# Gated linear attention, mixture of experts and a second layer on one core: k's decay and the weights' splitting on VectorE, the state's decay on ScalarE, and a fifth late unit of layer 2

## The chip, the core and the metric

The kernel runs on one core of a Trainium2 chip. TensorE (PE) multiplies matrices and loads its weights over a side path (PEld). VectorE (DVE), ScalarE (ACT) and GpSimd (POOL) work on tiles in SBUF or on PE's results in PSUM, and SyncE (SP) issues transfers. Each engine takes its instructions in the order of the program and waits on semaphores for the others. The metric is the device time of one execution in microseconds (us).

## The reference, cut to what matters

```python
# q, k, v, alpha: (4, 8, 768, 48)
for t in range(S):
    state = alpha[:, :, t, :, None] * state + einsum('bhd,bhe->bhde', k[:, :, t], v[:, :, t])
    y[:, :, t] = einsum('bhd,bhde->bhe', q[:, :, t], state)
x = y as (3072, 384)
# experts: only rows with x @ w_skip > 0
logits = x @ w_gate                   # 8 experts, the best one is taken
x = x + gate * (relu(x @ w1[e]) @ w2[e])      # 384 -> 1024 -> 384
# second layer, all rows
h = x @ w_in                          # 384 -> 2048
out = (h - tanh(h)) @ w_out           # 2048 -> 384
```

All of it is wanted to fp32 accuracy.

## The kernel before

**Attention.** The sequence is cut into 6 chunks of 128 steps, and with 4 batches that makes 24 units, one for each call of `astep(s)`. For unit s + 2 DVE scans the decay forward (`F`, L196) and backward (`G`, L203). POOL multiplies q by F (`qh`, L209), k by G (`kh`, L214) and makes `pf` (L218), the decay over the whole chunk. For unit s PE makes the scores `pa` (`mmA`, L226), which DVE masks (`am`, L231); it transposes `kh` (`trk`, L255), which ACT copies to `kt` (L261); it sums y in `py` from the old state (`mmYs`, L240) and from `am` (`mmYa`, L247); and it sums the new state in `pd` (`mmS`, L271 and L274). DVE multiplies `pd` by `pf` and so writes the state `st` (`evst`, L282), two instructions of 64 partitions for each unit. ACT copies y (`xT`, L288), PE transposes it back beside the routing scores (`mmX`, L295), and ACT copies both out (L303, L304). Routing sorts the rows of 12, 8 and 4 units by expert, and POOL's indirect transfers scatter them to `xb` in memory (L414).

**Weights.** PE multiplies rounded fp32 numbers, so every weight is split into a rounded high part (`wh`, by ACT) and the rest (`wl`), and each product is made of three. A unit is a 128x1536 block: 64 units are the experts', 16 are layer 2's. An expert's unit takes two operations: `wh` on ACT (L141), and `wl` (L144) on DVE, or on POOL for every fourth unit. A unit of layer 2 comes in 64 bits and takes seven: `cs` and `ca` on DVE (L155, L156), `cl` on ACT (L159), `cs` on DVE (L160), `wh` on ACT (L162), two multiplications and subtractions on POOL (L166, L167) and `wl` on DVE (L170). These four groups are called s0 to s3 in `wsplit`. Five units of layer 2 are split beside the attention, seven beside the experts, and the last four ("late") in the first steps of layer 2.

**Tail of attention, experts and layer 2.** Between attention and experts the first five units of layer 2 are already used for block 0. The experts' loop takes one unit in each step: `mm1` (L559, into `hp`), `hh` on ACT, `hl` on DVE (L564), and `mm2` two steps later (L577 to L579). Layer 2 goes over 6 blocks of 512 rows by 16 units less the five done: `mm1b` (L463, into `h`), then `g` by ACT and DVE (L469, L471), `gh` on ACT (L473), `gl` on DVE (L475), and two steps later `mm2b` (L497). Results leave by indirect transfers (L511).

The order is written by hand: lists `at` and `aft` hold what is to be issued ahead of a step and behind it, and every engine keeps that order.

Of the kernel before, what the change touches and what calls it, by code (L numbers as in the profile page):

```python
# [19 lines left out]
C = 128  # L20
# [22 lines left out]
NE0 = 5  # L43
NLATE = 4

# [15 lines left out]
@with_exitstack  # L61
def tile_kernel(ctx: ExitStack, tc: tile.TileContext, att0, att, vz, wsg, wmoe, wff, out):
    nc = tc.nc
# [62 lines left out]

    def wsplit(i, eng=None):
# [313 lines left out]
    def split2(nb, a, pt=None):  # L441
        d = X2[nb]
        if a == 0:
# [242 lines left out]
    def astep(s):  # L686
# [22 lines left out]
        if ok(s + 2):  # L709
            scanF(s + 2)  # L710
            mkqh(s + 2)
        trk(s)
        evk(s)
        if ok(s - 2):
            mmX(s - 2)
            evxa(s - 2)
        if ok(s - 1):
            mmYs(s - 1)
        mask(s)
        if ok(s - 1):  # L720
            evst(s - 1)
            mmYa(s - 1)
# [71 lines left out]
    for f in range(NE0):  # L794
# [7 lines left out]
        if f == NE0 - 1:  # L802
# [152 lines left out]
def layout(inputs):  # L955
# [24 lines left out]
    def units(w_in, w_out):  # L980
# [34 lines left out]
```

## Time and profile before

| | us |
|---|---|
| runs | 768.1, 770.59, 770.76 (median 770.59) |
| profiled execution | 771.64 |
| its span in the trace | 769.9 |
| PE busy | 696.4 (90%) |
| DVE busy | 473.5 (62%) |
| ACT busy | 280.8 (36%) |
| POOL busy | 257.2 (33%) |

The shares are averages over stages that look nothing alike. The span is best read in these stretches: the start up to 35.3 us, attention in its steady loop up to 163.5, its end with the routing and block 0's first part up to 212.85, the experts up to 365.86, layer 2 while its late units are split up to about 408, and layer 2 to the end. The rows below name each stage's engines with their busy time.

### The profile page before, as it was taken

To read this page: it belongs to the slowest core of one execution; us is meant where nothing else is said; L and a number is where in the kernel's file an instruction comes from. 1 tells how busy PE (TensorE), PEld (TensorE's weight loads), DVE (VectorE), ACT (ScalarE), POOL (GpSimd) and SP (SyncE) were. 2 spreads that over 40 slices of the span, in tenths; PEclk is the share of its full clock that TensorE was granted. 3 is DMA by queue.
4 is the path that set the end of the run, shared out by engine and by line. 5 is a ranking of instruction groups with operands and counts; after the bars stand their busy time and mean duration, and the time that the engine had idled before them with its cause. 6 is when DMAs were issued, how large, how long until landed. Compare 5 with 4: busy or idle time off the path is not lost.

```text
span 769.9 us, 11892 instructions
## 1 busy us (share of the span) xinstructions
PE 696.4 (90%) x4707; PEld 635.0 (82%) x4707; DVE 473.5 (62%) x698; ACT 280.8 (36%) x508; POOL 257.2 (33%) x196
## 2 busy tenths in 40 slices
PE   4788878857899998999999999999999999999993
PEld 3677767746798888989888989999989899989993
DVE  7999999883779988983775333433333343434331
ACT  2323313212475655663343333333333332333221
POOL 6687657954536754551430100200020020002002
PEclk9999989989999999999999999999999999999997
DMA  9899746524477876861311101100110020001001
GB/s 270 220 278 277 185 93 184 148 82 145 136 279 244 271 252 215 268 206 71 98 42 42 42 0 42 42 1 0 42 42 1 10 74 1 1 0 42 1 1 44
DMA packets 31598, 84.55 MB, mean 110 GB/s; under 512 B 4437, under 2 KB 12661, under 8 KB 31536
## 3 DMA queue, kind: packets, MB, share of 16 engines
q1 hardware_dynamic: 27440, 71.80, 31.5%
q0 software_dynamic: 4096, 11.92, 4.3%
q8 instruction: 39, 0.64, 0.4%
q14 instruction: 23, 0.19, 0.1%
HBM read 67.02 MB, written 17.43 MB: 110 GB/s over the span
## 4 chain that ended last, share of the span: by engine, by line
issue 47%; DVE 29%; PE 14%; POOL 4%; ACT 2%; DMA 2%; another core or an unknown queue 1%; POOLq 0%; DVEq 0%; ACTq 0%
DVE wl L144 5%; DVE F L196 4%; DVE G L203 4%; PE hp L559 4%; DVE am L231 2%; POOL out_dram L511 2%; DVE wl L170 2%; DVE st L282 1%; DVE hl L564 1%; DVE cs L155 1%; PE y L497 1%; PE pa L226 1%; PE yp L577 1%; DVE ca L156 1%; PE yp L579 1%
## 5 line engine op out<-in xcount | busy, mean ns | idle before, releaser
L471 DVE TENSOR_TENSOR g<-h,g 128x512 f32<-128x512 f32 x96 | 66.3, 691 | 161.4 <-ACT g L469 152.2
L511 POOL DMA_INDIRECT out_dram<-ob,id x24 | 23.4, 977 | 335.4 <-DVE ob L510 308.7
L497 PE MATMUL y<-wh,gl 128*128 128x384 f32 x384 | 131.0, 341 | 3.3 <-DVE gl L475 2.8
L497 PE MATMUL y<-wh,gh 128*128 128x384 f32 x384 | 130.2, 339 | 0.0
L497 PE MATMUL y<-wl,gh 128*128 128x384 f32 x384 | 130.1, 339 | 0.0
L475 DVE TENSOR_TENSOR gl<-g,gh 128x512 fp32r<-128x512 f32 x96 | 78.2, 814 | 65.9 <-ACT gh L473 44.0
L469 ACT ACTIVATE g<-h 128x512 f32<-128x512 f32 x96 | 57.3, 598 | 168.2 <-PE h L463 166.0
L463 PE MATMUL h<-xh,wh 128*128 128x512 f32 x288 | 115.5, 401 | 1.0 <-DVE g L471 1.0
L463 PE MATMUL h<-xl,wh 128*128 128x512 f32 x288 | 113.9, 395 | 0.0
L463 PE MATMUL h<-xh,wl 128*128 128x512 f32 x288 | 113.8, 395 | 0.0
L473 ACT CAST gh<-g 128x512 fp32r<-128x512 f32 x96 | 59.6, 620 | 83.4 <-DVE g L471 83.1
L497 PEld LDWEIGHTS y<-wh,gl 128*128 128x128 f32 x384 | 72.6, 189 | 5.2 <-DVE gl L475 5.1
L497 PEld LDWEIGHTS y<-wl,gh 128*128 128x128 f32 x384 | 72.6, 189 | 4.2
L497 PEld LDWEIGHTS y<-wh,gh 128*128 128x128 f32 x384 | 72.6, 189 | 3.9
L463 PEld LDWEIGHTS h<-xl,wh 128*128 128x128 f32 x288 | 54.3, 189 | 12.5
L559 PE MATMUL hp<-eh,wh 128*128 128x256 f32 x192 | 56.8, 296 | 8.4 <-DVE hl L564 8.0
L141 ACT CAST wh<-raw 128x768 fp32r<-128x768 f32 x64 | 53.4, 835 | 26.6 <-PE yp L579 18.5
L463 PEld LDWEIGHTS h<-xh,wh 128*128 128x128 f32 x288 | 54.3, 188 | 10.6 <-DVE g L471 1.9
L463 PEld LDWEIGHTS h<-xh,wl 128*128 128x128 f32 x288 | 54.5, 189 | 8.6
L144 DVE TENSOR_TENSOR wl<-raw,wh 128x768 fp32r<-128x768 f32 x45 | 61.2, 1360 | 0.0
L559 PE MATMUL hp<-eh,wl 128*128 128x256 f32 x192 | 53.8, 280 | 0.0
L559 PE MATMUL hp<-el,wh 128*128 128x256 f32 x192 | 53.7, 280 | 0.0
(139 smaller groups left out, 1273.3 us busy)
## 6 DMA issues: line engine op xcount, KB each, us to landing
raw<-in_wmoe_dram SPq DMA_DIRECT2D x64, 384.0 KB, 3.6
raw<-in_wff_dram SPq DMA_DIRECT2D x16, 768.0 KB, 4.9
it<-in_att_dram SPq DMA_DIRECT2D x40, 289.5 KB, 7.0
vt<-in_vz_dram SPq DMA_DIRECT2D x24, 256.0 KB, 3.0
xb<-zero SPq DMA_DIRECT2D x6, 776.0 KB, 10.7
rows<-xb SPq DMA_DIRECT2D x6, 776.0 KB, 4.4
xe<-xb SPq DMA_DIRECT2D x8, 388.0 KB, 4.7
it<-in_att_dram SPq DMA_DIRECT2D x2, 772.0 KB, 9.5
```

What stands on the lines that cost most here:

```text
L141: A.copy(t_["h"], raw_t[i])
L144: (eng or V).tensor_tensor(t_["l"], raw_t[i], t_["h"].bitcast(F32), ALU.subtract)
L196: V.tensor_tensor_scan(flat(d["F"]), d["it"][:, :NP * C], flat(ind), 0.0, ALU.mult, ALU.add)
L203: V.tensor_tensor_scan(flat(d["G"])[:, ::-1], d["it"][:, 1:NP * C + 1][:, ::-1], flat(d1s[u % 2])[:, ::-1], 0.0, ALU.mult, ALU.add)
L463: T.matmul(hp, *todo.pop(0), start=len(todo) == last, stop=not todo)
L469: A.activation(g, hp, AF.Tanh)
L471: V.tensor_tensor(g, hp, g, ALU.subtract)
L473: A.copy(gh, g)
L475: V.tensor_tensor(gl, g, gh.bitcast(F32), ALU.subtract)
L497: T.matmul(o, g_[:, sl_], w_[:, DM:], start=first and n == 0, stop=last and n == len(todo) - 1)
L511: s_ = nc.gpsimd.indirect_dma_start(out[:, :], bass.IndirectOffsetOnAxis(d["id"][:, a:a + 1], 0), ob, None, bounds_check=N - 1, oob_is_err ...
L559: T.matmul(hp, w_[:, ks], x_[:, k], start=n == 0, stop=n == 3 * KT - 1)
```

## The change

`kh` is made by DVE instead of POOL. `pf` stays on POOL, now directly behind `qh` (`mkpf`). All `wl` of the experts and both operations of s2 are on DVE, so that POOL keeps `qh`, `pf` and the indirect transfers. `evst` leaves DVE: ACT multiplies `pd` by the column of `pf`, four activations of 128x112 for each unit. For that `pd` and the two `py` become PSUM tiles that are zeroed once and stay, and v is no longer padded from 48 to 64 columns. In a step `mmYs(s - 1)` comes ahead of `trk(s)`, and `evst(s - 1)` ahead of `evk(s)`. The zeros of `xb` are written by four transfers at steps 6 to 9 instead of six at steps 2 to 7. Beside the experts six units of layer 2 are split, one for every nine steps, instead of seven, one for every seven; five are late, with s2 and s3 in the same step.

```diff
-NLATE = 4
+NLATE = 5
@@ wsplit
         def n1():
-            (eng or V).tensor_tensor(t_["l"], raw_t[i], t_["h"].bitcast(F32), ALU.subtract)
+            V.tensor_tensor(t_["l"], raw_t[i], t_["h"].bitcast(F32), ALU.subtract)
...
         def s2():
             a_ = t_["a"].bitcast(F32)
-            G.tensor_tensor(t_["f"], t_["f"], t_["s"].bitcast(F32), ALU.mult)
-            G.tensor_tensor(a_, a_, t_["h"].bitcast(F32), ALU.subtract)
+            V.tensor_tensor(t_["f"], t_["f"], t_["s"].bitcast(F32), ALU.mult)
+            V.tensor_tensor(a_, a_, t_["h"].bitcast(F32), ALU.subtract)
@@ mkkh
-        G.tensor_tensor(d["kh"], d["kk"], d["G"], ALU.mult)
+        V.tensor_tensor(d["kh"], d["kk"], d["G"], ALU.mult)
+
+    def mkpf(u):
+        d = U[u]
@@ evst
-            for j in range(2):
-                r = slice(HP * j, HP * j + HP)
-                V.tensor_tensor(st[u % B][r, :, HP * j:HP * j + D], d["pd"][r],
-                                d["pf"][r].unsqueeze(2).to_broadcast([HP, NP, D]), ALU.mult)
+            for p in range(NP):
+                A.activation(st[u % B][:, p, :HP + D], pd[:, p, :HP + D], AF.Copy, scale=d["pf"][:, p:p + 1])
@@ astep
         if ok(s + 2):
             scanF(s + 2)
             mkqh(s + 2)
+            mkpf(s + 2)
+        if ok(s - 1):
+            mmYs(s - 1)
         trk(s)
+        if ok(s - 1):
+            evst(s - 1)
         evk(s)
...
-        if ok(s - 1):
-            mmYs(s - 1)
         mask(s)
         if ok(s - 1):
-            evst(s - 1)
             mmYa(s - 1)
@@ stages beside the experts
-        stage(NMU + r, 7 * (r - NE0) + 5, None, max(0, 7 * (r - NE0) + -1))
+        stage(NMU + r, 9 * (r - NE0) + 5, max(0, 9 * (r - NE0) - 1))
@@ late units
-        for n, f_ in zip((0, 0, 1, 2), wsplit(r)):
+        for n, f_ in zip((0, 0, 1, 1), wsplit(r)):
```

Three places show how it moves instructions. First DVE in an attention step that carries a part of a layer-2 unit. Before:

```order
L196 SCALAR_TENSOR_TENSOR F_1007<-it_97,ind 128x512
L197 RECIPROCAL d_1_105<-F_1007 128x4
L231 TENSOR_TENSOR am_1031<-pa_996,maskT 128x1024
L282 TENSOR_TENSOR st_124<-pd_979,pf_835 64x4x48 x2
L203 SCALAR_TENSOR_TENSOR G_1043<-it_97,d_0_104 128x512
L160 TENSOR_SCALAR cs_974<-ca_975 128x768
L196 SCALAR_TENSOR_TENSOR F_1082<-it_98,ind 128x512
```

DVE after, in a step of the same kind:

```order
L196 SCALAR_TENSOR_TENSOR F_722<-it_97,ind 128x512
L197 RECIPROCAL d_0_104<-F_722 128x4
L234 TENSOR_TENSOR am_751<-pa_711,maskT 128x1024
L203 SCALAR_TENSOR_TENSOR G_761<-it_97,d_0_104 128x512
L214 TENSOR_TENSOR kh_763<-it_97,G_761 128x512
L160 TENSOR_SCALAR cs_689<-ca_690 128x768
L166 TENSOR_TENSOR cl_691<-cl_691,cs_689 128x768
L167 TENSOR_TENSOR ca_690<-ca_690,wh_767 128x768
L196 SCALAR_TENSOR_TENSOR F_798<-it_98,ind 128x512
```

The two `st` are gone from DVE; `kh` stands directly behind G, and L166 and L167 between L160 and the next F.

Second, ACT in an attention step. Before:

```order
L288 COPY xT_861<-py_814 128x512
L261 COPY kt_873<-pk_868 128x512
L303 COPY xr_316<-px_875 128x384
L304 COPY l_317<-px_875 128x36
L288 COPY xT_930<-py_882 128x512
```

ACT after:

```order
L289 COPY xT_796<-py_128 128x512
L284 ACTIVATE st_121<-pd,pf_581 128x112 x4
L264 COPY kt_818<-pk_809 128x512
L304 COPY xr_326<-px_820 128x384
```

Four activations that write the state now stand between `xT` and `kt`.

Third, DVE in two steps of layer 2 with a late unit (`g_8`, `g_9` are the units' numbers). Before:

```order
L471 TENSOR_TENSOR g_8_4335<-h_0_8_4325,g_8_4335 128x512
L475 TENSOR_TENSOR gl_8_4337<-g_8_4335,gh_8_4336 128x512
L448 COPY id_4356<-rows_2903 128x4
L439 TENSOR_TENSOR xl_1_4355<-px_0_4358,xh_1_4354 128x3x128
L170 TENSOR_TENSOR wl_4288<-ca_4281,cl_4282 128x768
L155 TENSOR_SCALAR cs_4367<-raw_4365 128x768
L156 SCALAR_TENSOR_TENSOR ca_4368<-raw_4365,cs_4367 128x768
L160 TENSOR_SCALAR cs_4367<-ca_4368 128x768
L471 TENSOR_TENSOR g_9_4387<-h_0_9_4377,g_9_4387 128x512
L475 TENSOR_TENSOR gl_9_4389<-g_9_4387,gh_9_4388 128x512
```

DVE after:

```order
L155 TENSOR_SCALAR cs_4352<-raw_4350 128x768
L156 SCALAR_TENSOR_TENSOR ca_4353<-raw_4350,cs_4352 128x768
L160 TENSOR_SCALAR cs_4352<-ca_4353 128x768
L472 TENSOR_TENSOR g_9_4372<-h_0_9_4362,g_9_4372 128x512
L476 TENSOR_TENSOR gl_9_4374<-g_9_4372,gh_9_4373 128x512
L166 TENSOR_TENSOR cl_4354<-cl_4354,cs_4352 128x768
L167 TENSOR_TENSOR ca_4353<-ca_4353,wh_4359 128x768
L170 TENSOR_TENSOR wl_4360<-ca_4353,cl_4354 128x768
L472 TENSOR_TENSOR g_10_4404<-h_0_10_4394,g_10_4404 128x512
```

L166 and L167 now stand on DVE ahead of L170, and all three ahead of the second step's `g`, not behind its `gl`.

## Rows read from the trace of the kernel before

**Rows 1.** Windows: length, busy (instructions) of PE, PEld, DVE, ACT, POOL, clock, DMA, GB/s.

```profile
35.30:163.50 128.20, 99.07 (x1234) 89.88 (x1235) 123.24 (x157) 37.09 (x81) 96.22 (x72) 0.93 0.70 185
...
212.85:365.86 153.01, 144.63 (x1004) 138.88 (x1004) 128.03 (x167) 88.51 (x155) 76.77 (x43) 1.00 0.68 225
365.86:408.30 42.44, 40.90 (x199) 34.69 (x199) 32.14 (x41) 18.28 (x30) 16.80 (x10) 1.00 0.20 63
```

**Rows 2.** Timeline of an attention step: start, duration, engine, line, operation, idle before.

```profile
65.98 1.16 PE L226 MATMUL pa<-qh,kh 64*128 64x128 f32 x16
...
66.31 1.43 POOL L214 TENSOR_TENSOR kh<-it,G 128x512 f32<-128x512 f32 x1 [2.09 <-DVE G L203]
66.53 2.30 DVE L196 TENSOR_TENSOR_SCAN F<-it,ind 128x512 f32<-128x512 f32 x1
...
69.08 1.23 DVE L231 TENSOR_TENSOR am<-pa,maskT 128x1024 f32<-128x1024 f32 x1
...
72.00 1.16 PE L226 MATMUL pa<-qh,kh 64*128 64x128 f32 x16
```

**Rows 3.** DVE's groups in 35.3:163.5: count, busy us, mean ns, idle before.

```profile
L196 DVE TENSOR_TENSOR_SCAN F<-it,ind 128x512 f32<-128x512 f32 x18 | 37.7, 2094 | 0.0
L203 DVE TENSOR_TENSOR_SCAN G<-it,d 128x512 f32<-128x512 f32 x18 | 30.0, 1666 | 0.5
...
L282 DVE TENSOR_TENSOR st<-pd,pf 64x192 f32<-64x192 f32 x34 | 11.9, 351 | 2.1 <-PE py L240 1.8
L156 DVE SCALAR_TENSOR_TENSOR ca<-raw,cs 128x768 uint32<-128x768 uint32 x5 | 8.6, 1720 | 0.2
```

**Rows 4.** Three lines' instructions: ns min/median/max, first and last start.

```profile
L196 DVE TENSOR_TENSOR_SCAN F<-it,ind x24: 1192/1222/7539, 3.5 to 153.4; 128x512 f32<-128x512 f32 x24
...
L144 DVE TENSOR_TENSOR wl<-raw,wh x45: 942/949/3849, 215.3 to 353.2; 128x768 fp32r<-128x768 f32 x45
...
L475 DVE TENSOR_TENSOR gl<-g,gh x96: 691/693/6101, 194.7 to 753.3; 128x512 fp32r<-128x512 f32 x96
```

**Rows 5.** ACT's smallest copy out of PSUM in 35.3:163.5.

```profile
L304 ACT COPY l<-px 128x36 f32<-128x36 f32 x18 | 3.5, 195 | 0.0
```

**Rows 6.** Window of five us around a wait of PE, columns as in the first group.

```profile
105.00:110.00 5.00, 2.63 (x35) 2.45 (x35) 4.80 (x14) 0.00 (x0) 1.63 (x2) 0.53 0.59 105
```

**Rows 7.** Timeline: three waits of PE or DVE, in attention and in its tail.

```profile
107.37 0.91 PE L271 MATMUL pd<-st,ident 128*64 128x192 f32 x4 [4.53 <-DVE st L282]
...
170.83 0.55 PE L436 MATMUL px<-ident,rows 128*128 128x128 f32 x3 [2.13 <-DMA rows<-xb]
...
198.65 6.10 DVE L475 TENSOR_TENSOR gl<-g,gh 128x512 fp32r<-128x512 f32 x1 [0.69 <-ACT gh L473]
```

**Rows 8.** Timeline of the experts: DVE and POOL at 248, and hl near the end.

```profile
247.55 2.56 POOL L167 TENSOR_TENSOR ca<-ca,wh 128x768 f32<-128x768 f32 x1
...
248.33 0.41 DVE L564 SCALAR_TENSOR_TENSOR hl<-hp,hh 128x256 fp32r<-128x256 f32 x1
...
250.85 0.41 DVE L564 SCALAR_TENSOR_TENSOR hl<-hp,hh 128x256 fp32r<-128x256 f32 x1
...
361.19 0.43 DVE L564 SCALAR_TENSOR_TENSOR hl<-hp,hh 128x256 fp32r<-128x256 f32 x1 [1.69 <-ACT hh L563]
...
363.30 0.42 DVE L564 SCALAR_TENSOR_TENSOR hl<-hp,hh 128x256 fp32r<-128x256 f32 x1 [1.69 <-ACT hh L563]
```

**Rows 9.** Timeline of layer 2: DVE beside the late units, PE at the eleventh step.

```profile
366.59 0.55 DVE L155 TENSOR_SCALAR cs<-raw 128x768 uint32<-128x768 uint32 x1
...
375.97 0.55 DVE L155 TENSOR_SCALAR cs<-raw 128x768 uint32<-128x768 uint32 x1
...
380.29 2.16 DVE L475 TENSOR_TENSOR gl<-g,gh 128x512 fp32r<-128x512 f32 x1 [0.69 <-ACT gh L473]
...
385.75 0.56 DVE L155 TENSOR_SCALAR cs<-raw 128x768 uint32<-128x768 uint32 x1
...
408.30 0.47 PE L463 MATMUL h<-xh,wh 128*128 128x512 f32 x1
```

More of the change, by code (lines that the diff above doesn't have):

```diff
@@ L61, in tile_kernel @@
 @with_exitstack
-def tile_kernel(ctx: ExitStack, tc: tile.TileContext, att0, att, vz, wsg, wmoe, wff, out):
+def tile_kernel(ctx: ExitStack, tc: tile.TileContext, att0, att, vt, wsg, wmoe, wff, out):
     nc = tc.nc
@@ L125, in wload, with wsplit @@
             nc.sync.dma_start(raw_t[i].rearrange("p a b -> p (a b)"), wff[i - NMU].bitcast(U32))
-    def wsplit(i, eng=None):
+    def wsplit(i):
         own = (ring if i % RING < RING0 else rings["ring2"]) if i < NMU else ffE if i < NMU + NE0 else None
@@ L188, in vload @@
     def vload(u):
-        U[u]["vt"] = w2.tile([128, H, HP], F32, tag="vt", name=f"vt{u}", bufs=4)
-        nc.sync.dma_start(U[u]["vt"], vz[u].rearrange("p (h e) -> p h e", h=H))
+        U[u]["vt"] = w2.tile([128, H, D], F32, tag="vt", name=f"vt{u}", bufs=4)
+        nc.sync.dma_start(U[u]["vt"], vt[u].rearrange("p (h e) -> p h e", h=H))
     def scanF(u):
@@ L236, in mmYs @@
         d = U[u]
-        d["py"] = psY(f"py{u}", u % 2).rearrange("p (a t) -> p a t", a=NP)
+        d["py"] = pys[u % 2]
         if u >= B:
@@ L266, in mmS @@
         if u < NU - B:
-            d["pd"] = psS(f"pd{u}", 1)[:, :NP * D].rearrange("p (a e) -> p a e", a=NP)
             rs = [slice(HP * j, HP * j + HP) for j in range(2)]
+            es = [slice(HP * j, HP * j + D) for j in range(2)]
             if u >= B:
-                for r in rs:
-                    T.matmul(d["pd"][r], ident[:, r], st[u % B][:, :, r.start:r.start + D], start=True, stop=False)
+                for r, e in zip(rs, es):
+                    T.matmul(pd[r, :, e], ident[:, r], st[u % B][:, :, e], start=True, stop=False)
             for p in range(NP):
-                for j, r in enumerate(rs):
-                    T.matmul(d["pd"][r, p], d["kt"][:, p, r], d["vt"][:, 2 * p + j, :D],
+                for j, (r, e) in enumerate(zip(rs, es)):
+                    T.matmul(pd[r, p, e], d["kt"][:, p, r], d["vt"][:, 2 * p + j],
                              start=p == 0 and u < B, stop=p == NP - 1)
@@ L447, in split2 @@
             d["id"] = cp.tile([128, 4], U32, tag="id", name=f"id{nb}", bufs=2)
-            V.tensor_copy(d["id"], d["r"][:, :, CID].bitcast(U32))
+            V.tensor_scalar(d["id"], d["r"][:, :, CID].bitcast(U32), N, None, ALU.min)
         ts_ = slice(128 * a, 128 * a + 128)
@@ L624, in tile_kernel @@
     st = [w1.tile([PR, NP, PR], F32, name=f"st{b}") for b in range(B)]
+    pd = psS("pd", 1).rearrange("p (a e) -> p a e", a=NP)
+    V.memset(pd, 0.0)
+    pys = [psY(f"py{i}", i).rearrange("p (a t) -> p a t", a=NP) for i in range(2)]
     zero = w1.tile([128, RW], F32, name="zero")
@@ L627, in tile_kernel @@
     mkqh(0)
+    mkpf(0)
     scanG(0)
     mkkh(0)
+    for t_ in pys:
+        V.memset(t_, 0.0)
     G.memset(zero, 0.0)
@@ L652, in tile_kernel @@
     mkqh(1)
+    mkpf(1)
     scanG(1)
@@ L673, in tile_kernel @@
     at[1].append(consts2)
-    for s in range(2, 2 + (NS + NIN) // 512):
-        r0 = 512 * (s - 2)
+    for s in range(6, 6 + NS // 512):
+        r0 = 512 * (s - 6)
         at[s].append(lambda r0=r0: nc.sync.dma_start(
@@ L689, in ok, with pX_ @@
             return 0 <= u < NU
-        def py_(name):
-            return psY(name, s % 2)
+        def pX_(name):
+            return ps["T"].tile([128, 512], F32, tag=f"X{s % 2}", name=name)
         if ok(s + 4):
@@ L733, in astep @@
         if c1 is not None:
-            route2(c1, py_)
+            route2(c1, pX_)
     aload(3)
@@ L812, in tile_kernel @@
                 xprep(0, a)
-            for f_ in wsplit(RING0, G):
+            for f_ in wsplit(RING0):
                 f_()
@@ L816, in tile_kernel @@
         if f < RING0:
-            for f_ in wsplit(f, G):
+            for f_ in wsplit(f):
                 f_()
@@ L827, in tile_kernel, with stage @@
     aft[0].append(partial)
-    def stage(i, step, eng, ld):
+    def stage(i, step, ld):
         at[ld].append(lambda: wload(i))
-        for k, f_ in zip((0, 1, 2, 4), wsplit(i, eng)):
+        for k, f_ in zip((0, 1, 2, 4), wsplit(i)):
             at[step + k].append(f_)
@@ L835, in tile_kernel @@
         s_ = j - LA
-        stage(j, s_, V if j % 4 else G, max(0, s_ - RAWS + 1))
+        stage(j, s_, max(0, s_ - RAWS + 1))
     for r in range(NE0, NF2 - NLATE):
-        stage(NMU + r, 7 * (r - NE0) + 5, None, max(0, 7 * (r - NE0) + -1))
+        stage(NMU + r, 9 * (r - NE0) + 5, max(0, 9 * (r - NE0) - 1))
     for e in range(1, NE):
@@ L973, in layout @@
     rows[..., AQ + NP * C:] = pairs(inputs["k"]).reshape(NU, 2, D, NP * C)
-    vz = np.zeros((NU, C, H, HP), f)
-    vz[..., :D] = inputs["v"].reshape(B, H, NC_, C, D).transpose(2, 0, 3, 1, 4).reshape(NU, C, H, D)
+    vt = inputs["v"].reshape(B, H, NC_, C, D).transpose(2, 0, 3, 1, 4).reshape(NU, C, H, D)
     wsg = np.zeros((2, HP, NP, 9), f)
@@ L990, in layout @@
         "att": rows[ITS:],
-        "vz": vz.reshape(NU, 128, H * HP),
+        "vt": vt.reshape(NU, 128, DM),
         "wsg": wsg.reshape(PR, NP, 9),
```

2 lines of the change are left out of this document (1 added, 1 removed).

## The prediction

> **What bounds the kernel now.** I read the windows by stage first. In attention's steady loop DVE is busy 123.2 of 128.2 us, PE 99.1 and POOL 96.2: DVE sets the pace. Beside the experts PE is busy 144.6 of 153.0 and DVE 128.0. In layer 2, while its late units are split, PE has 40.9 of 42.4 [rows 1], and afterwards it never stops for long.
>
> Then I asked whether DVE's time is work or waiting. The timeline shows the same form at two lengths. F takes 2.30 us at 66.53, where POOL's `kh` runs from 66.31 to 67.74 [rows 2]; F ends 1.09 us after `kh`, nearly its whole own length. Its shortest of 24 is 1.19, its median 1.22, and one took 7.54; `wl` of the experts between 0.94 and 3.85, `gl` between 0.69 and 6.10 [rows 4]. The 2.16 us `gl` in layer 2 [rows 9] is of the same kind. So an instruction of DVE that reads two tiles of SBUF waits until a tensor operation of POOL is over, and that wait is counted as its busy time. Those that read PSUM do not: `am` takes 1.23 behind that F [rows 2], `hl` 0.41 to 0.43 [rows 8].
>
> **Attention's loop, 18 steps.** What goes: F averages 2.094 where it needs 1.21, so 18 x 0.88 = 15.9 us of waiting; G 1.666 against 1.22 (F's median; G is the same scan backward), 18 x 0.45 = 8.0; `ca` 1.720 against about 0.96 (five, the unhindered length by the 0.94 of `wl`, the same 128x768), 3.8 [rows 3, 4]. Together 27.7. `st` leaves DVE: 11.9 [rows 3]. What comes: `kh`, a 128x512 product of two SBUF tiles, by the shortest `gl` 0.69 [rows 4]: 18 x 0.69 = 12.4. L166 and L167, 128x768, by the shortest `wl` 0.94: five units, 10 x 0.94 = 9.4. Net: -27.7 - 11.9 + 12.4 + 9.4 = -17.8. POOL keeps `qh` and `pf`. They run behind F, beside the reciprocal and `am`, which reads PSUM, so I leave 1.3 us for collisions with G: **-16.5**.
>
> Where does the saving stop? The next limit is PE. One of its steps, pa to pa, is 6.02 us at 65.98 to 72.00 [rows 2], and by the windows 99.07 / 18 = 5.5 of a step are busy. The forecast makes 128.2 - 16.5 = 111.7, 6.2 a step: DVE and PE then run close to each other, and PE doesn't stop the gain short of -20 or so. ACT takes four activations of 128x112. Its 128x36 copy out of PSUM takes 0.195 [rows 5]; more columns make that about 0.26, so 1.04 us a step, on an engine that is busy 37.1 of 128.2 [rows 1]. But they stand ahead of `kt`, and PE's `mmS` at the end of the step waits for `kt`. By the order the wait begins after `mmYs`, some 2.1 us into PE's step, then 1.04 and `kt`'s 0.6, together 3.8, while `mmS` comes at about 4.6: hidden by `mmX` and `mmYa`. If an activation took 0.6 instead, the chain would end at 5.1, past that, and a step would be about 6.2 at best with nothing over for DVE's own waits. That is the first rival; the term's range is -20 to -8.
>
> The row shows a copy, and no row an activation with a column as its scale. The Trainium skill, "ScalarE: Activation LUTs", section "What ACT_TABLE_LOAD costs", gives 186 ns plus 0.833 ns an element with constants and some 93 ns more for each pointer operand, with an overlap of 93 ns from one to the next. An estimate by that page is 0.28 us for each, 1.1 a step; the sum would not move, since the chain would end 0.1 us later, still ahead of `mmS`.
>
> **The start.** DVE loses there the waits of two G and one `ca` and gains six `kh`, three pairs of `st` fewer, and two 128x512 fills. By the prices above: about -1 x 3 + 6 x 0.69 - 3 x 0.7 + 2 x 0.5, near zero, and the first `kh` is ready earlier because it takes half as long. The zeros of `xb` leave this part. I take **-1**, between -3 and +1.
>
> **Attention's tail.** PE waits 2.13 us for rows at 170.83, whose scatters stand behind L166 and L167 on POOL; and a `gl` at 198.65 takes 6.10 instead of 0.69 beside three `wl` on POOL [rows 7]. After, DVE has five `wl` of 0.94 there instead, in steps where it has room. I take **-1.5** (0 to -3) and **-2** (0 to -5.4).
>
> **Experts.** At 248 to 251 `hl` follows `hl` after 2.52 us, with a `wl` between that POOL's L167 held until 250.11; near the end, with hardly anything on DVE but `hl`, after 2.11 (361.19 to 363.30) [rows 8]. PE in full flow would need 64 x 2.11 = 135 and some 7 for the transposes of tokens, 142 of the 153.0. All of DVE's work, nine units, would be after: nine `hl` and `wl`, 9 x (0.42 + 0.94) = 12.2, one layer-2 unit with six 128x768 operations, at most 6 x 0.94 = 5.6, and tokens' 128x384 parts, some 2: 19.8 as a bound from above by durations, which overlap at their ends, against PE's 9 x 2.11 + 0.9 = 19.9. It fits, barely, and `hl` may stand behind a burst of 0.94 pieces: **-9.5**, between -11 and -5 (zero is the second rival).
>
> **Layer 2's late units.** This is where I expect a loss. A pair of steps is set by DVE: from `cs` at 375.97 to `cs` at 385.75 are 9.78 us, the first `cs` is at 366.59 [rows 9]. After, `gl` isn't held (2.16 to 0.69: -1.47), and two operations come (2 x 0.94, with their overlap 2 x 0.87 = 1.74): 10.1 a pair; the first has no `xl`, 9.6. So the fifth unit's `cs` comes at 366.59 + 9.6 + 3 x 10.14 = 406.6. Its `wl` ends behind `cs`, `ca`, `cs`, `g`, `gl` and the three operations, some 7.7 us later, 414.2. The eleventh step's `mm1b`, which takes this unit, starts before the change at 408.30 [rows 9], and all that follows on PE stands behind it. PE then waits 5.9 us. Waiting has a second price: after 4.53 us without work at 107.37 [rows 7] the granted clock of the five us around was 0.53 [rows 6], the lower of the two levels, 1.2 GHz instead of 2.4; I add 2. **+8**, between 0 and +12: the low end if PE reaches that step so late that the unit is ready.
>
> **The sum.** The profiled execution took 771.64 us (span 769.9 and 1.7 around it). 771.64 - 16.5 - 1 - 1.5 - 2 - 9.5 + 8 = 749.1. It lies 1.05 above the median of the runs, 770.59; so I predict **748.1** for the median.
>
> **Rivals.**
> - ACT's state update bounds attention: `mmS` waits for `kt` behind four activations. For it: `kt` has only 0.8 us to spare by the count above. Against: ACT is busy 29% of the loop. It halves attention's gain to -8: 756.6.
> - The experts gain nothing: DVE's longer bursts, now 0.94 pieces of a layer-2 unit between `hl` and `hl`, hold PE as POOL's lock did. For it: the count of 19.8 against 19.9. Against: these are durations, not spacings. Without -9.5: 757.6.
> - The fifth late unit is hidden, because PE comes later to the eleventh step or the pairs run shorter. Without +8: 740.1.
> - Slower: the long DVE instructions are not POOL's doing but DVE's own (memory, PSUM), and stay long. Then DVE only gets more work: in attention + 12.4 + 9.4 - 11.9 = +9.9, beside the experts 19 `wl` and 6 x 2 operations, 31 x 0.94 = 29, of which the 25 that DVE has to spare [rows 1] hide perhaps half, +15, and the late units +15, since with `gl` still long a pair takes 9.78 + 1.74 = 11.5: 771.64 + 9.9 + 15 + 15, about 810 for the median. It decides if F in the new trace is still near 2 us with `qh` alone on POOL. Against it: no row of `hl` and `am` shows it, and the long F ends its own length after POOL's operation.
> - PE's own pace sets attention and the experts already, so that what DVE saves becomes its idle time, the start, tail and late units cancel, and nothing is left: 770. Against it: PE's busy time leaves 29 us of the loop [rows 1].
>
> **Chances.** Forecast 0.70, ACT's chain 0.11, experts without gain 0.08, hidden late unit 0.05, no effect 0.03, slower 0.03. The range holds the forecast's own bounds and the first three rivals: 738 to 760. A measurement of this kernel can tell about 0.5% from no change, 3.9 us: faster means under 766.7. That holds for the forecast and three rivals: 0.94; same 0.03; slower 0.03.
>
> **What would show it.** In the profile after, F should be near 1.2 us and G near 1.25 in every step, POOL busy below half of before, a step of PE near 6.0 to 6.2, and PE's waits in the loop for `am` or `kh`, not for `kt`. ACT's `st` should take 0.25 to 0.3 each. Beside the experts `hl` should follow `hl` after 2.2. In layer 2 a wait of PE for `wl` of the fifth late unit, 4 to 7 us long, should stand ahead of its eleventh step, and half clock behind it. I am wrong if F stays long (then the lock isn't POOL's), if `kt` arrives after `mmYa`, or if the eleventh step starts without a wait.

## The result and the profile after

The changed kernel took 738.23 us (median of four runs, 735.21 to 740.0) against 770.13 of the kernel before: a ratio of 0.9586, 95% interval 0.9549 to 0.9623. The forecast was 748.1 with a range of 738 to 760: the right sign and the right terms, but almost a third of the gain missing. The time lies 0.2 us above the low end of the range, and one of the four runs, 735.21, lies below it. The profiled spans, 769.9 and 736.8, differ by 33.1 us; by stages, with the bounds taken at the same instructions in both traces:

| stage | before | after | difference | forecast |
|---|---|---|---|---|
| start, to the seventh F | 35.3 | 33.4 | -1.9 | -1 |
| attention's loop, to the end of the last G | 128.3 | 107.6 | -20.6 | -16.5 |
| tail, to the first `mm1` | 49.3 | 40.1 | -9.2 | -3.5 |
| experts, to the end of the last `xe` | 153.8 | 143.7 | -10.2 | -9.5 |
| layer 2 | 403.3 | 412.0 | +8.7 | +8 |

The first view is the windows by stage of the changed kernel: length, busy time of PE, PEld, DVE, ACT and POOL with counts, granted clock, share of DMA, GB/s.

```profile
33.40:141.03 107.63, 91.23 (x1230) 84.72 (x1228) 104.87 (x150) 54.25 (x145) 53.53 (x44) 0.99 0.83 207
...
181.10:323.94 142.84, 141.49 (x1004) 139.43 (x1003) 118.42 (x191) 86.64 (x153) 15.64 (x14) 1.00 0.71 236
323.94:368.47 44.53, 41.36 (x199) 34.77 (x199) 34.42 (x50) 18.01 (x30) 2.25 (x2) 1.00 0.24 78
```

Against [rows 1], DVE is still the busiest engine of the loop, 104.9 of 107.6, with PE at 91.2 behind it. Beside the experts PE is busy 141.5 of 142.8: there it is the bound now, at the 142 that the forecast gave as its floor. DVE's groups in the loop (count, busy us, mean ns, idle before):

```profile
L203 DVE TENSOR_TENSOR_SCAN G<-it,d 128x512 f32<-128x512 f32 x18 | 24.0, 1335 | 0.0
L196 DVE TENSOR_TENSOR_SCAN F<-it,ind 128x512 f32<-128x512 f32 x18 | 21.9, 1219 | 0.0
...
L214 DVE TENSOR_TENSOR kh<-it,G 128x512 f32<-128x512 f32 x17 | 11.8, 692 | 0.6
L156 DVE SCALAR_TENSOR_TENSOR ca<-raw,cs 128x768 uint32<-128x768 uint32 x5 | 4.8, 959 | 0.2
L166 DVE TENSOR_TENSOR cl<-cl,cs 128x768 f32<-128x768 f32 x5 | 4.8, 958 | 0.9 <-ACT st L284 0.5
L167 DVE TENSOR_TENSOR ca<-ca,wh 128x768 f32<-128x768 f32 x5 | 4.8, 951 | 0.0
```

F averages 1.219, with 1.217 to 1.225 in its 18 calls, where [rows 3] had 2.094; `ca` is at 0.959 where it had 1.720. G averages 1.335 where it had 1.666: 16 of its 18 calls take 1.22 to 1.27, the other two 1.94 and 2.20. `kh` at 0.692 and the two operations of s2 at 0.95 cost what the nearest rows said.

In layer 2 the loss stands where it was expected, ahead of the eleventh step's product with the fifth late unit's low part. The timeline of PE there, and the granted clock of the four us behind it:

```profile
368.47 0.51 PE L464 MATMUL h<-xh,wh 128*128 128x512 f32 x1 [0.60 <-DVE g L472]
372.58 0.79 PE L464 MATMUL h<-xh,wl 128*128 128x512 f32 x1 [3.60 <-DVE wl L170]
373.17 0.63 PE L464 MATMUL h<-xl,wh 128*128 128x512 f32 x1
373.60 0.63 PE L464 MATMUL h<-xh,wh 128*128 128x512 f32 x1
```

```profile
372.50:376.50 4.00, 3.92 (x10) 3.15 (x11) 1.78 (x4) 1.04 (x3) 0.00 (x0) 0.50 0.00 0
```

PE waits 3.60 us for `wl` and then runs at 0.50, the 1.2 GHz level, where its matmuls follow each other after 0.43 us. Before, PE went into this step at 408.30 [rows 9] without such a wait.

### The profile page after: what moved, and what is told of

It reads as the page before. It is cut to its first block, busy times and chain, and to the rows that moved or that the text cites. A ratio compares the mean times of both kernels' runs of the same rounds, so it can differ in the third digit from the quotient of the medians.

```text
span 736.8 us, 11897 instructions
## 1 busy us (share of the span) xinstructions
PE 686.1 (93%) x4707; PEld 629.2 (85%) x4707; DVE 449.8 (61%) x736; ACT 301.7 (41%) x588; POOL 125.3 (17%) x121
## 4 chain that ended last, share of the span: by engine, by line
issue 55%; PE 26%; DVE 12%; POOL 3%; ACT 1%; DMA 1%; POOLq 0%; ACTq 0%; SPq 0%; DVEq 0%
PE hp L560 8%; PE yp L578 3%; PE yp L579 3%; PE yp L580 3%; DVE G L203 2%; POOL out_dram L512 2%; DVE F L196 2%; PE pa L229 2%; DVE am L234 2%; PE py L243 2%; PE px L296 1%; PE h L464 1%; PE py L250 1%; DVE kh L214 1%; POOL qh L209 1%
## 5 line engine op out<-in xcount | busy, mean ns | idle before, releaser
L476 DVE TENSOR_TENSOR gl<-g,gh 128x512 fp32r<-128x512 f32 x96 | 66.5, 693 | 65.9 <-ACT gh L474 44.0
L464 PEld LDWEIGHTS h<-xh,wh 128*128 128x128 f32 x288 | 54.4, 189 | 14.5 <-DVE g L472 5.8
L229 PE MATMUL pa<-qh,kh 64*128 64x128 f32 x384 | 30.8, 303 | 27.9 <-POOL qh L209 19.5
```

Source lines behind the costliest of these rows:

```text
L229: T.matmul(d["pa"][:, j, p], d["kh"][r, p], d["qh"][r, p], start=p == 0, stop=p == NP - 1)
L464: T.matmul(hp, *todo.pop(0), start=len(todo) == last, stop=not todo)
L476: V.tensor_tensor(gl, g, gh.bitcast(F32), ALU.subtract)
```

## The experiments

Each kernel's ratio is to the kernel before, run on the same chip in between, since the chips differ by some us; the time beside it is the kernel's own median. Lengths of stages come from one profiled execution of each kernel. The loops of late4 and best, which the edits don't touch, are 109.0 and 109.7 us long against 107.6, so 2 us in the loop are within what changes by itself.

| kernel | time, us | ratio | 95% interval |
|---|---|---|---|
| the change | 738.2 | 0.9586 | 0.9549 to 0.9623 |
| late4 | 731.9 | 0.9519 | 0.9487 to 0.9550 |
| kh_pool | 744.6 | 0.9688 | 0.9653 to 0.9723 |
| st_dve | 752.7 | 0.9792 | 0.9758 to 0.9827 |
| mask_first | 759.5 | 0.9875 | 0.9843 to 0.9908 |
| mask_first_qh_dve | 749.3 | 0.9703 | 0.9652 to 0.9755 |
| s2_pool | 750.9 | 0.9737 | 0.9701 to 0.9773 |
| s2_last_pool | 752.5 | 0.9723 | 0.9672 to 0.9773 |
| wl_pool | 748.1 | 0.9700 | 0.9679 to 0.9721 |
| before_kh_dve | 771.7 | 1.0000 | 0.9968 to 1.0031 |
| before_wl_dve | 763.5 | 0.9895 | 0.9858 to 0.9933 |
| before_s2_dve | 769.5 | 0.9937 | 0.9909 to 0.9965 |
| best | 731.6 | 0.9448 | 0.9416 to 0.9480 |

The theory, called the lock below: an instruction of DVE that reads two tiles of SBUF stands still while POOL's tensor operation runs; attention and the experts gain by what POOL gives up, and layer 2 loses by the fifth late unit. The rival: DVE's long instructions have another cause, and only DVE's amount of work counts.

### One part of the change undone: kh, the state's decay

kh_pool is the changed kernel with one letter different:

```diff
-        V.tensor_tensor(d["kh"], d["kk"], d["G"], ALU.mult)
+        G.tensor_tensor(d["kh"], d["kk"], d["G"], ALU.mult)
```

> The changed kernel with kh back on POOL, behind qh and pf. If a DVE instruction that reads two SBUF tiles waits for POOL's tensor operation, F goes back from 1.22 us to about 2 in most steps: 18 x 0.8 more for F, 18 x 0.61 less for kh, so about 742, and PE waits for kh as well. If the long F had another cause, F stays at 1.22 and the time falls by what kh costs DVE, to 728 to 732.

It takes 744.6 us, a little above the 742 of the theory. DVE's groups in its loop:

```profile
L203 DVE TENSOR_TENSOR_SCAN G<-it,d 128x512 f32<-128x512 f32 x18 | 27.5, 1527 | 0.0
L196 DVE TENSOR_TENSOR_SCAN F<-it,ind 128x512 f32<-128x512 f32 x18 | 25.0, 1387 | 0.0
...
L156 DVE SCALAR_TENSOR_TENSOR ca<-raw,cs 128x768 uint32<-128x768 uint32 x5 | 11.4, 2283 | 0.2
L166 DVE TENSOR_TENSOR cl<-cl,cs 128x768 f32<-128x768 f32 x5 | 11.4, 2277 | 0.6 <-ACT cl L159 0.2
```

DVE loses 11.8 us of `kh` and gets 3.5 on G, 3.1 on F and 6.6 each on `ca` and `cl`: less work of its own, and a loop 5.8 us longer (113.5 against 107.6). But the wait did not go to F as I had written: only three F are long (2.29), and the ten `ca` and `cl`, two-input instructions that come while POOL works, take it (two of them, at 3.7 and 4.0, stand behind `qh` and `kh` in a row). Where F had started first, it kept its length and POOL's `kh` was the longer one, 2.04 us instead of about 1.3:

```profile
67.48 1.19 DVE L196 TENSOR_TENSOR_SCAN F<-it,ind 128x512 f32<-128x512 f32 x1
67.70 2.04 POOL L214 TENSOR_TENSOR kh<-it,G 128x512 f32<-128x512 f32 x1
```

st_dve puts the state's decay back on DVE, in the old place:

```diff
-            for p in range(NP):
-                A.activation(st[u % B][:, p, :HP + D], pd[:, p, :HP + D], AF.Copy, scale=d["pf"][:, p:p + 1])
+            for j in range(2):
+                r, e = slice(HP * j, HP * j + HP), slice(HP * j, HP * j + D)
+                V.tensor_tensor(st[u % B][r, :, e], pd[r, :, e],
+                                d["pf"][r].unsqueeze(2).to_broadcast([HP, NP, D]), ALU.mult)
```

> The changed kernel with the state's decay back on DVE behind the mask, two instructions a unit as before, in place of ACT's four. If DVE sets the pace of attention, it pays up to 17 x 0.74 = 12.6 us: about 748. If PE and ACT's chain (four activations ahead of kt) set it, DVE has room and ACT is relieved: 736 or less.

It takes 752.7, more than the 748 expected; the loop takes 120.6 us, 13.0 more. The rows of DVE's work and, from the table of waits (us in total, times, the longest), of PE's:

```profile
L203 DVE TENSOR_TENSOR_SCAN G<-it,d 128x512 f32<-128x512 f32 x18 | 22.0, 1223 | 0.5
...
L285 DVE TENSOR_TENSOR st<-pd,pf 64x192 f32<-64x192 f32 x34 | 11.9, 350 | 0.4 <-PE py L243 0.2
```

```profile
PE pd L274 <- DVE st L285: 17.4, 10, 3.2
```

`st` costs its full 11.9 us and PE waits for it again, so DVE sets the pace and not ACT. ACT's price for the same work, by the line of its activations (ns least, median, most):

```profile
L284 ACT ACTIVATE st<-pd,pf x80: 337/354/367, 14.0 to 130.6; 128x112 f32<-128x112 f32 x80
```

Four of them take 1.09 us together in the timeline, (1.09 - 0.354) / 3 = 0.25 from one to the next; the forecast had 0.26. The estimate by the Trainium skill, "ScalarE: Activation LUTs", section "What ACT_TABLE_LOAD costs", was 0.28; the trace is slightly under it, and the measured spacing decides.

### What covers POOL's remaining product

After the change POOL still makes `qh` in each step, and G hardly feels it. The timeline of one step of the changed kernel:

```profile
57.29 1.20 DVE L234 TENSOR_TENSOR am<-pa,maskT 128x1024 f32<-128x1024 f32 x1
57.30 1.30 POOL L209 TENSOR_TENSOR qh<-it,F 128x512 f32<-128x512 f32 x1 [3.46 <-ACT kt L264]
...
58.41 1.27 DVE L203 TENSOR_TENSOR_SCAN G<-it,d 128x512 f32<-128x512 f32 x1
```

PE's waits in the whole loop are these:

```profile
PE pa L229 <- POOL qh L209: 16.2, 10, 3.3
PE pa L229 <- DVE am L234: 0.2, 1, 0.2
```

PE waits ahead of `pa` and nowhere else, and never for `kt`. The profile puts the 16.2 us down to `qh`; I read it as waits for `am`, which ends at the same time, and tried to bring `am` forward. mask_first:

```diff
+        mask(s)
         if ok(s + 2):
             scanF(s + 2)
             mkqh(s + 2)
             mkpf(s + 2)
...
-        mask(s)
```

> The changed kernel with am(s) ahead of F(s + 2) on DVE instead of behind F and its reciprocal. In the changed kernel PE waits 19.5 us in all at pa, put down to POOL's qh; but pa at 65.41 follows the end of am (64.07 to 65.27) as closely as that of qh (64.07 to 65.34), and pa has a single buffer. If am is the releaser, the waits in steps with a weight unit shrink by 1.2 to 1.4 us each and the time falls by 6 to 10: about 730. If qh is, F and qh only come 1.2 us later, and the time rises by 0 to 5: 738 to 743.

Both were wrong: 759.5 us, 21 slower, the loop 125.5. The same step's place there, and the group in the loop:

```profile
65.79 1.21 DVE L196 TENSOR_TENSOR_SCAN F<-it,ind 128x512 f32<-128x512 f32 x1
...
67.14 1.27 POOL L209 TENSOR_TENSOR qh<-it,F 128x512 f32<-128x512 f32 x1 [4.59 <-issue]
67.25 2.23 DVE L203 TENSOR_TENSOR_SCAN G<-it,d 128x512 f32<-128x512 f32 x1
```

```profile
L203 DVE TENSOR_TENSOR_SCAN G<-it,d 128x512 f32<-128x512 f32 x18 | 38.9, 2160 | 0.6
L234 DVE TENSOR_TENSOR am<-pa,maskT 128x1024 f32<-128x1024 f32 x18 | 21.9, 1217 | 0.0
```

`qh` starts when F is done. What DVE does next runs beside it: `am`, one input from PSUM and one from SBUF, is not held; G, two inputs from SBUF, waits out the whole of `qh` and takes 2.16. `am` had been G's cover. If so, the cure is to take `qh` from POOL, though that gives DVE more work. mask_first_qh_dve:

```diff
-        G.tensor_tensor(d["qh"], d["qq"], d["F"], ALU.mult)
+        V.tensor_tensor(d["qh"], d["qq"], d["F"], ALU.mult)
```

> The kernel with am ahead of F (which took 759.5 us, with G 2.24 us long in nearly every step) and qh moved to DVE as well, so that POOL has no tensor operation of 128x512 in attention. DVE gets 24 x 0.61 = 14.6 us more work. If what am had covered was POOL's qh, G falls back to 1.22 and the time falls by 18 x (1.0 - 0.61) to 24 x 0.4, to about 750; if am's place itself is bad for DVE or PE, the added work lengthens it to 770 or more.

It takes 749.3 us, as expected, and by ratio 0.9703 against 0.9875. DVE in its loop:

```profile
L203 DVE TENSOR_TENSOR_SCAN G<-it,d 128x512 f32<-128x512 f32 x18 | 21.9, 1217 | 0.0
...
L209 DVE TENSOR_TENSOR qh<-it,F 128x512 f32<-128x512 f32 x18 | 11.9, 662 | 0.0
```

11.9 us more of work on the busiest engine, and the loop is 10.9 us shorter (114.5). G's fall from 2.16 to 1.217 shows the lock with nothing changed but the engine that makes `qh`. How much of the loop's gain comes from `qh` being ready sooner is not separated. The Trainium skill, "SBUF — State Buffer", section "Who interferes with whom", states it so: a DVE instruction with two SBUF inputs contends with a GpSimd instruction that reads SBUF, one with at most one such input, outside VectorE's 2-port performance modes, does not. The rows of `am` and G agree. "Two inputs" is not the whole class, though. In the kernel before, `cs`, which has a single SBUF input and takes 0.55 us elsewhere, took 2.20 beside a `wl` on POOL and ended 0.4 us after it, while no `hl` (896 in the 14 traces) took over 0.43 and no `am` (336) over 1.23:

```profile
326.35 2.25 POOL L144 TENSOR_TENSOR wl<-raw,wh 128x768 fp32r<-128x768 f32 x1 [3.13 <-ACT wh L141]
326.83 2.20 DVE L155 TENSOR_SCALAR cs<-raw 128x768 uint32<-128x768 uint32 x1
```

### The weights' splitting: wl and s2

wl_pool is the changed kernel with 19 of the experts' 64 `wl` on POOL again:

```diff
-            V.tensor_tensor(t_["l"], raw_t[i], t_["h"].bitcast(F32), ALU.subtract)
+            (G if i < RING0 + 1 or i % 4 == 0 else V).tensor_tensor(t_["l"], raw_t[i], t_["h"].bitcast(F32), ALU.subtract)
```

> The changed kernel with 19 of the 64 experts' wl back on POOL, the same as before the change (the first five, then every fourth). Attention is untouched: its loop should stay at 107.6 us. By the lock, the tail pays 2 to 5 us again (gl behind three wl, 6.1 us long) and the experts' stretch of 140.3 us rises by 4 to 8: about 746. If DVE sets the pace beside the experts by its work, 19 x 0.87 us less there make it faster: 732 or less.

748.1 us. The 6.1 us `gl` of [rows 7] is back, the tail is 3.4 us longer (43.5), the experts 3.1 (146.8), less than the 4 to 8 expected (from 143.7, not the 140.3 that the expectation names); the loop, which the edit doesn't touch, came out 1.9 longer (109.5):

```profile
172.80 6.10 DVE L476 TENSOR_TENSOR gl<-g,gh 128x512 fp32r<-128x512 f32 x1 [0.69 <-ACT gh L474]
```

s2_pool is the changed kernel with both operations of s2 there:

```diff
-            V.tensor_tensor(t_["f"], t_["f"], t_["s"].bitcast(F32), ALU.mult)
-            V.tensor_tensor(a_, a_, t_["h"].bitcast(F32), ALU.subtract)
+            G.tensor_tensor(t_["f"], t_["f"], t_["s"].bitcast(F32), ALU.mult)
+            G.tensor_tensor(a_, a_, t_["h"].bitcast(F32), ALU.subtract)
```

> The changed kernel with both operations of s2 (L166, L167) back on POOL, for all 16 units of layer 2. If POOL's tensor operations hold DVE, each unit holds F, G or wl for up to 3.7 us instead of taking 1.74 of DVE: five units in attention, some +2 each, six beside the experts, +0.5 to 1 each, and in layer 2 the fifth unit's wl waits for POOL behind gl, +2: 750 to 757. If DVE's time is all that counts, 16 x 1.74 us leave it and the time falls below 735.

750.9 us. The expectation's sum holds, its places do not: the loop is only 0.9 us longer (108.6), the experts 2.1, layer 2 shorter by 2.8 (409.2), and 10.1 us are lost in the tail (50.2). To see which unit does that, s2_last_pool leaves POOL the two operations of one unit alone, the last of the five that are split beside attention. The second operation changes in the same way.

```diff
-            V.tensor_tensor(t_["f"], ...)
+            (G if i == NMU + NE0 - 1 else V).tensor_tensor(t_["f"], ...)
...
```

> The changed kernel with L166 and L167 on POOL for one unit only, the fifth, whose operations fall into attention's last steps. All of the 10 us that the tail grew by with all of them on POOL (50.2 against 40.1) should come from this unit, because its operations stand ahead of scatters on POOL, and block 0's rows are loaded behind these: PE's wait for rows (7.4 us there) and ACT's wait for px that has no visible releaser (3.9 us) should both come back, tail 48 to 50, total about 747. If the tail's loss comes from the other units or from POOL's work beside the experts, the tail stays at 40 and the total at 738 to 740.

752.5 us, the tail 57.0: more than the 747 and 50 expected. POOL, PE and ACT in its timeline:

```profile
138.27 2.73 POOL L167 TENSOR_TENSOR ca<-ca,wh 128x768 f32<-128x768 f32 x1
141.16 1.28 POOL L415 DMA_INDIRECT xb<-xr,loc  x1 [0.16 <-issue]
142.74 0.97 POOL L415 DMA_INDIRECT xb<-xr,loc  x1 [0.30 <-issue]
```

```profile
149.75 0.90 PE L437 MATMUL px<-ident,rows 128*128 128x128 f32 x3 [7.43 <-DMA rows<-xb]
```

```profile
168.39 0.48 ACT L304 COPY xr<-px 128x384 f32<-128x384 f32 x1 [8.88 <-remote]
```

So the fifth unit's two operations stand ahead of attention's last scatters on POOL, the rows of block 0 are loaded behind these, and PE waits 7.4 us for them. In the kernel before that was 2.13 [rows 7], in the changed kernel it is nothing. All five profiled kernels with this unit's operations on POOL have the wait, 2.1 to 8.6 us long, and none of the nine others. The third row, 8.9 us in which ACT waits for no engine that the profile knows, is another matter (below).

### One part alone, from the kernel before

before_kh_dve, before_wl_dve and before_s2_dve each make one of the moves, with nothing else:

```diff
# before_kh_dve
-        G.tensor_tensor(d["kh"], d["kk"], d["G"], ALU.mult)
+        V.tensor_tensor(d["kh"], d["kk"], d["G"], ALU.mult)
# before_wl_dve
-            (eng or V).tensor_tensor(t_["l"], raw_t[i], t_["h"].bitcast(F32), ALU.subtract)
+            V.tensor_tensor(t_["l"], raw_t[i], t_["h"].bitcast(F32), ALU.subtract)
# before_s2_dve
-            G.tensor_tensor(t_["f"], t_["f"], t_["s"].bitcast(F32), ALU.mult)
-            G.tensor_tensor(a_, a_, t_["h"].bitcast(F32), ALU.subtract)
+            V.tensor_tensor(t_["f"], t_["f"], t_["s"].bitcast(F32), ALU.mult)
+            V.tensor_tensor(a_, a_, t_["h"].bitcast(F32), ALU.subtract)
```

> The kernel before with the experts' wl all on DVE. Attention stays at 128.2 us in its loop. The 6.1 us gl of the tail goes back to 0.69, -2 to -5, and the experts' stretch falls by 3 to 6 of the 10 that the whole change brought there: about 763. If the lock is not the cause, DVE's 19 x 0.87 = 16.5 us more lengthen the experts: 775 to 785.

763.5 us, ratio 0.9895: the experts' stretch falls from 153.8 to 146.0, more than expected, the loop hardly (127.0), the tail by 1.1.

> The kernel before with kh alone moved to DVE. F should lose the wait behind kh (18 x 0.88) and keep a wait only in steps with L166 and L167; qh then runs beside am, and G is free in most steps. Against that 24 x 0.61 us of kh on DVE: net -8 to -12, about 760. The waits of ACT for px at 182.7 and 187.7 in the tail (8.6 us, put down to no engine) stay, if they belong to the kernel before as it is laid out, and go if they come from what POOL does.

771.7 us, no gain (ratio 1.0000). Most of F's wait went, but the time did not follow. DVE from 35 to 165 us, and two waits of PE:

```profile
L203 DVE TENSOR_TENSOR_SCAN G<-it,d 128x512 f32<-128x512 f32 x18 | 26.9, 1494 | 0.5
L196 DVE TENSOR_TENSOR_SCAN F<-it,ind 128x512 f32<-128x512 f32 x18 | 23.2, 1289 | 0.0
...
L214 DVE TENSOR_TENSOR kh<-it,G 128x512 f32<-128x512 f32 x18 | 15.7, 870 | 0.6
L282 DVE TENSOR_TENSOR st<-pd,pf 64x192 f32<-64x192 f32 x34 | 11.9, 351 | 6.2 <-PE py L240 5.9
```

```profile
PE pd L271 <- DVE st L282: 21.0, 12, 5.0
...
PE px L436 <- DMA rows<-xb: 7.3, 1, 7.3
```

F loses 14.5 us of [rows 3] and G 3.1; `kh` brings 15.7 (0.870 each, where the unhindered length is 0.692). DVE's busy time in the loop falls by 7.4 us, to 115.9, but its idle time rises from 5.0 to 9.7, most of it in front of `st`, and the loop falls by only 2.7. In this profile the tail takes more than that back: 7.3 us for rows, and ACT's wait again (7.4). The profiled execution took 777.5, 5.7 above the median, so a typical run need not lose as much there.

> The kernel before with L166 and L167 on DVE for all 16 units, nothing else. The tail should fall from 49.3 by the wait for rows (2.1) and, if ACT's wait without a releaser belongs to POOL's part in the tail, by 4 to 5 more, to 42 to 44; attention's loop by 2 to 5, since F and ca lose the longest waits but DVE gets 10 x 0.87; the experts by 1 to 3; layer 2's late pairs stay within 2. Total 755 to 762. If DVE's work alone counted, 16 x 1.74 us more would make it slower: 780.

769.5 us, ratio 0.9937: less than expected. The tail falls by 2.6, the experts by 1.7, but the loop is 2.4 us longer (130.6). DVE's work is not the reason: its busy time there fell by 3.2, to 120.1, and its idle time rose from 5.0 to 10.5. It waits for PE ahead of `st`, and PE waits for `st`:

```profile
L282 DVE TENSOR_TENSOR st<-pd,pf 64x192 f32<-64x192 f32 x34 | 11.9, 351 | 5.4 <-PE py L240 5.1
```

```profile
PE pd L271 <- DVE st L282: 23.9, 13, 3.6
```

So in attention the moves are worth more together than one by one. `kh` alone takes 2.7 us off the loop and s2 alone adds 2.4; st_dve, which has both and `st` still on DVE, is 7.7 below the kernel before, and `st`'s leaving brings the other 13.0. Part of the saved work returned as these two engines' waits for each other; why it does so less with both moves made is not shown, and the change's other edits to attention (narrower v, the place of `mmYs`, fewer zeros) have no run of their own.

### The fifth late unit, and a faster kernel

late4 differs from the changed kernel in one line:

```diff
-NLATE = 5
+NLATE = 4
```

> The changed kernel with four late units instead of five (seven split beside the experts, one every nine steps), nothing else. If layer 2 lost about 9 us to the fifth late unit (in the changed kernel PE's first matmul on its low part comes at 372.58 after a wait of 3.6, and the stretch from the first cs to the eleventh step is 47.9 us where it was 41.7), that stretch returns to about 41 and the time falls to about 730, with up to 1.5 us given back beside the experts for one more unit's 4.6 us on DVE. If the loss has another cause (DVE's two added operations in each pair of steps), only some 2 us come back: 736.

731.9 us, ratio 0.9519. From the last `xe` to the eleventh step 42.9 us pass instead of 43.7, and the rest takes 361.8 instead of 368.3. The experts do not notice the seventh unit (143.5). So 7.3 of the 8.7 us are the fifth unit's. The other 1.4 would be the two operations added to each pair of steps, but before_s2_dve, which adds them alone, has a layer 2 only 0.3 longer, and the seven kernels with five late units, their operations on DVE, differ by 1.5 among themselves: that share is not shown.

best keeps four late units and moves their operations on DVE from ahead of `g` into the gap between `g` and `gl`, where DVE waits for `gh`:

```diff
-            collections.deque(after(), 0)
+            ch = after()
+            for _ in range(3):
+                next(ch)
+            for f_ in mid[i]:
+                f_()
+            collections.deque(ch, 0)
...
```

> The changed kernel with four late units instead of five, and in layer 2's first steps a late unit's operations stand between g and gl on DVE, where it waits 0.69 us for gh, instead of ahead of g. With four late units alone: 731.9, a pair of steps 10.1 us, PE waiting 0.3 to 0.7 for g in each. If g held PE, the pairs shrink toward PE's 8.5 and the time falls by 1 to 2: 730. If gl becomes the one that PE waits for, it stays at 732 or rises by 1 to 2.

It has the lowest ratio, 0.9448 (0.9416 to 0.9480), and its interval doesn't touch late4's; by its own median, 731.6, it is level, on a chip where the kernel before took 773.3 instead of 769.0. So it is the faster one if a ratio carries from one chip to the other; the two never ran on the same chip. DVE in two pairs of steps:

```profile
333.71 0.55 DVE L155 TENSOR_SCALAR cs<-raw 128x768 uint32<-128x768 uint32 x1
...
335.77 0.68 DVE L476 TENSOR_TENSOR gl<-g,gh 128x512 fp32r<-128x512 f32 x1
...
341.12 0.55 DVE L155 TENSOR_SCALAR cs<-raw 128x768 uint32<-128x768 uint32 x1
...
349.02 0.55 DVE L155 TENSOR_SCALAR cs<-raw 128x768 uint32<-128x768 uint32 x1
```

A pair takes 7.4 to 7.9 us on DVE instead of the 9.8 of [rows 9], `gl` waits for nothing any more, and the eleventh step comes 38.1 us after the last `xe`: 4.8 earlier than in late4. Its profiled tail was 5 us longer than late4's (44.1 against 39.1), with ACT's unexplained wait in it.

## Why the prediction was right where it was, and where it fell short

The steps of the prediction were right; that the number fell inside the range, by 0.2 us, was partly luck, since two stages gained more than their own ranges allowed: attention (-20 to -8) and the tail (0 to -8.4 from both its terms). The start, -1, measured -1.9, is inside its range; which of its parts did that has no run.

**The lock.** Right, as a mechanism and in size: F and `ca` lost 15.8 and 3.8 us in the loop, as the step had it (15.9 and 3.8), G 6.0 of 8.0. mask_first against mask_first_qh_dve shows it apart from the other moves. The step named too few instructions: `cs` with one SBUF input was held as well. I had named the cover, `am` beside `qh`, in half a sentence, and did not see that everything hangs on it until mask_first took it away.

**Attention, -16.5; measured -20.6.** The terms of the sum measured -15.8 (F), -6.0 (G), -3.8 (`ca`), -11.9 (`st`), +11.8 (`kh`, with one of its 18 outside the window) and +9.6 (L166 and L167): together -16.1, where -17.8 less the allowance of 1.3 made -16.5. So the allowance was not too large: G's two long calls and its small excess cost 2.0. What the sum put at nothing is the rest. DVE's busy time fell by 123.2 - 104.9 = 18.4, 2.3 more than the terms, part of it on `am` (-0.5) and on the routing's `lg` and `dl` (-1.6). Its idle time fell by another 2.2, from 5.0 to 2.8; the 2.1 us of idle in front of `st` that [rows 3] show left the engine with `st`. That ACT's chain wouldn't bind was right: PE never waits for `kt` in the loop, and st_dve shows DVE as the bound.

**The tail, -3.5; measured -9.2.** The two terms named were right: PE's wait for rows is gone (2.1), and `gl` is 0.69 again, worth about 2.0 from the tail's third `mm1b` to its end (21.9 to 19.9); wl_pool puts 3.4 back. The other 5.1 us were gained ahead of that third `mm1b`, where two waits of ACT for `px` stand in the kernel before; the prediction had no term for them. ACT in the tail, before:

```profile
182.68 0.48 ACT L303 COPY xr<-px 128x384 f32<-128x384 f32 x1 [4.67 <-remote]
187.70 0.48 ACT L303 COPY xr<-px 128x384 f32<-128x384 f32 x1 [3.97 <-remote]
```

and the same two after:

```profile
155.66 0.48 ACT L304 COPY xr<-px 128x384 f32<-128x384 f32 x1 [1.95 <-PE px L296]
157.95 0.48 ACT L304 COPY xr<-px 128x384 f32<-128x384 f32 x1 [1.23 <-PE px L296]
```

PE had finished `px` at 179.94 and ACT took it at 182.68; PE then waited 2.9 us, by the order for ACT's next copy (the profile names no releaser), and ran at half clock behind it. I first put this down to POOL's part in the tail, because it is in s2_pool and s2_last_pool and in the four traces of the kernel before and its variants. That fell: mask_first_qh_dve and best, which have the changed kernel's tail, show 7.1 and 4.4 us of it, wl_pool, with POOL busier there, none, and late4, kh_pool, st_dve and mask_first none. It comes and goes between kernels with the same tail, from 0 to 7.1 us. late4, kh_pool, st_dve, mask_first and the changed kernel, without it, have tails of 38.3 to 40.1 us, the two with it 42.0 and 44.1: some 2 to 6 us. What releases ACT there is open, and how much of the measured 32 us is owed to its absence can't be settled from one profile of each kernel.

**Experts, -9.5; measured -10.2.** Right. PE is now busy 141.5 of 142.8, so the second rival (bursts of 0.95 on DVE hold `hl`) did not come: the count by durations, 19.8 against 19.9, was the bound from above that it was called. In the runs, `wl` alone brought 7.8 (before_wl_dve), s2 alone 1.7.

**Layer 2, +8; measured +8.7.** Right in place and size, with its parts a little different. The fifth `cs` stood at 364.78, 40.1 behind the first, where 40.0 was forecast (the working gives 9.78 - 1.47 + 1.74 = 10.05 a pair, not the 10.14 that its sum takes; the traced pairs after the first are 10.1 to 10.2). PE came to the eleventh step 2.1 us later than forecast, because it waited 3.1 us in all for `g` on the way instead of 1.0, so it waited 3.6 us for `wl` instead of 5.9. The half clock cost about 2.3, where 2 was assumed: from `wl` to the next step PE took 6.3 us, in late4 4.0. late4 gives back 7.3 of it.

**The rivals.** ACT as the bound, the hidden late unit, no effect and the slower one are refuted, in this order, by st_dve, late4, the ratio, and F's 1.219. That several of the change's parts bring little by themselves (before_kh_dve nothing, before_s2_dve 0.6%) shows how near the no-effect rival was for any one of them.

## What to carry to other kernels

Look at one instruction form at two lengths before you move work off a busy engine: if the longer ones end with another engine's operation, moving that operation can pay, even onto the busy engine itself (mask_first_qh_dve). One such move may bring nothing while others of the kind remain (before_kh_dve). An operation that remains on the other engine needs cover, here a DVE instruction that reads PSUM, and such a pair must be kept together when the order is changed. Work that is needed late should stand in the gaps of a dependent chain (between `g` and `gl`), not ahead of it.

## What the runs showed of the hardware

- A DVE product with one input in PSUM ran at full speed beside a POOL product (1.20 us beside `qh`), while a scan with two SBUF inputs took 2.16 instead of 1.22 at the same place.
- The wait goes to the DVE instruction with two SBUF inputs that comes while POOL works: in kh_pool `ca` and `cl` averaged 2.28 instead of 0.96, and F only 1.39. Where DVE's had started first, POOL's waited (`kh` 2.04 instead of about 1.3).
- A TENSOR_SCALAR with one SBUF input was held too: `cs` took 2.20 beside a POOL operation of 2.25, instead of 0.55.
- ACT's copies in the tail waited up to 8.9 us with no visible releaser in 8 of 14 profiled kernels, and not in the other six.
